# Four PSUM banks in one tile, one ScalarE copy for each unit, and eight absolute values moved from VectorE to ScalarE

## The chip, the core and the metric

The kernel runs on one core of one Trainium2 chip. A core has five engines that run side by side, each through its own list of instructions in order: TensorE (PE in the profile; its weight loads are PEld), VectorE (DVE), ScalarE (ACT), GpSimd (POOL) and SyncE (SP). They wait for each other through semaphores. The metric is the device time of one execution in microseconds (us): the median of three runs before was 1696.31 us (1691.14 to 1697.28).

## What is computed

One block with two parts, on 2048 tokens of width 576: a state-space convolution (the kernel of it is made from 128 complex poles for each channel, and applied by FFT), and a gated MLP.

```python
P = jnp.exp(logdA[:, :, None] * l[None, None, :])
K = jnp.einsum("dn,dnl,dn->dl", Cc, P, dB).real
...
Yf = Uf * Kf[None, :, :, :]
y = irfft2(Yf, (1, L2))[:, :, 0, :L] + u * Dskip
...
x = x + ga * _A_ref(h, ...)      # h: layer norm of x, modulated
h = _layernorm(x) * (1 + cb) + sb
z = gelu(h @ w_in); g = w_sp @ layernorm(z2) + b_sp
x = x + gb * ((z1 * g) @ w_out)
```

## The kernel before, in words

The function `ssm` makes the first part (about the first 385 us), `Mlp.phase_a` and `Mlp.phase_b` the second, a long stretch of float16 matrix products. The change touches `ssm` alone.

`ssm` is cut into small units, each a Python generator: a call runs it to its next `yield`, which records a few instructions on one or two engines. The text `ORDER` lists the calls, and nothing else sets the order: `t5 e9 k4` means the next step of `t_unit(5)`, `e_unit(9)`, `kg_unit(4)`. All instructions go through `Pin`, which keeps every engine in that order. The units:

- `poles` (O, P), `mod_unit` (M), `ln_stats` (S), `ln_rows` (R): the poles and the modulation rows, and the layer norm of the input. They stand early.
- `ln_half` (A, 16 of them): the first FFT step of half the channels of two token blocks. It writes four PSUM banks (`pk`), then copies each bank into `st1o`, 128 x 288, by a ScalarE instruction of its own (lines 552 to 554), with a `yield` behind each.
- `e_unit`, `t_unit`, `p_unit`, `kg_unit`, `k1_unit` (e, t, p, k, 1; 36 each): amplitudes (Exp), phases (Sin), their products on VectorE, the sum over poles on TensorE, and its first FFT step. In `t_unit` TensorE leaves phases in `ps` (two banks). For 25 of the 36 (`ROUNDED`) the rounding is done on TensorE; then VectorE takes the absolute value from PSUM into `ct` (line 603), ScalarE takes Sin of `ps` into `f`, and Sin of `ct` with a bias of a quarter turn. `p_unit` multiplies both on VectorE with the amplitudes.
- `u_unit`, `z_unit`, `v_unit`, `y_unit` (u, z, v, y): FFT of the input, the product in the frequency domain (VectorE), the way back, and the residual. `k1_unit` and `v_unit` write two banks and copy each by a ScalarE instruction of 128 x 256; `mod_unit` does so with 128 x 288, twice.

PSUM has eight banks. `ps` takes four, as two tiles of two banks. The other four are `pk_a` to `pk_d`, one tile each; `ps1()` hands them out, and the digits of `PLAN["pk"]` say which one comes next. A matmul that writes a bank waits until the last reader of that bank is done.

Of the kernel before, what the change touches and what calls it, by code (L numbers as in the profile page):

```python
# [9 lines left out]
F32 = mybir.dt.float32  # L10
# [4 lines left out]
ALU = mybir.AluOpType  # L15
# [15 lines left out]
COPIED = set()  # L31
# [6 lines left out]
    "pk": "01230123230123012301230120123012301231023102310232102130213021302130213021302301230122301230123012312031203120"  # L38
        "31203120312031203103201320323012302310231023103210321031203120132012031231201230123012032012031203120321021021"
        "30230123013021032103210321321031021032130130213021320123120312012301230123023102310231032103210123012301230213"  # L40
        "021320312031230123012310312031203120312031320120312031203123013021300101010101010101010101010101010101010101",
# [9 lines left out]
ON_ACT = set()  # L51
# [3 lines left out]
B0 O0 O0 O0 O0 B2 O0 O0 O0 O0 B7 O0 B1 O0 O0 O0 B6 O0 O0 O0 O0 O0 O0 x0 O0 O0 O0 O0 P0 S0 O0 S0 B3 O0 O0 i2 O0 O0 O0 P0 M2 O0 O0 S0 S0 B4 P0 S0 O0 Q0 P0 e1 S0 M2 e1 i1 e0  # L55
P0 P0 g0 e1 e0 P0 e0 e1 P0 t1 t2 i0 g1 O0 M2 e0 P0 M1 t1 t2 t1 P0 P0 t0 w3 P0 M1 t0 M2 t1 t0 t2 M1 M0 M1 M0 t0 e2 j1 R1 P0 p1 M3 t2 M0 p1 M3 R0 e2 R3 e6 p1 M0 B5 e2 M0 e6
M3 w4 k1 e4 e2 P0 M3 k1 O0 P0 e3 11 p0 e4 11 e6 M4 M0 e5 p0 P0 p0 e6 S1 S1 p2 M4 k0 M4 p2 11 R2 p2 e5 k0 e5 S1 M0 M3 M0 P0 k2 M4 e5 M0 P0 t5 k2 A0 e3 A0 S1 A0 A0 A0 w5 t5
S1 e3 P0 e3 A0 t3 S1 A1 t5 A1 A1 r2 A1 P0 t3 R4 A1 t7 A0 R5 A1 A2 A2 O0 P0 t3 t3 A2 A2 t4 P0 A1 A2 A2 A3 p3 A2 A3 t5 P0 r3 A3 A3 t4 t4 j2 M4 10 10 e4 A3 A3 A3 e4 12 p3 12
e7 p3 e7 P0 e7 R7 t7 10 R6 P0 p5 S2 12 k3 e8 e7 O0 k3 e8 A4 S2 A4 S2 A4 e8 S2 A4 A4 A4 e8 p5 P0 A5 t4 A5 A5 P0 A5 p5 A5 p4 A5 t7 a4 A4 A5 t6 A6 A6 A6 p4 A6 t6 A6 p4 A6 t8
A7 A7 P0 t7 A7 A7 O0 k4 A6 P0 S2 A7 13 t6 p7 A7 k4 t8 p7 R9 14 13 O0 k5 P0 P0 a5 t6 14 14 t8 p7 Q1 13 t8 M5 x3 k7 P0 e11 R8 A7 k5 M5 S3 k7 S3 A8 A8 e11 R11 e9 A8 e10 e11  # L60
P0 e9 e11 P0 p6 S3 S3 A8 P0 A8 R10 t10 A8 e10 A9 t10 A9 A9 A9 p8 p8 r6 e10 A9 A9 t9 e10 t10 A10 A8 P0 A10 A10 A10 A9 t11 p6 A10 A10 17 P0 t10 M5 p6 17 k6 M5 p8 t11 t9 17
k6 A11 A11 r7 S3 t11 t11 e12 A11 A11 Q2 15 R13 A11 A11 A10 p11 k8 t9 15 15 R12 A11 k8 A12 p11 A12 e12 A12 p11 A12 e14 A12 t14 A12 A13 e14 p10 A13 t14 A13 R15 e9 p10 A13
p10 A13 R14 A13 e9 t14 A12 e12 t12 e12 A14 A14 t9 A14 t15 A14 A14 t12 A13 t14 A14 t12 A15 A15 t14 O0 O0 A15 e16 k10 P0 A15 P0 A15 16 A15 P0 O0 p9 t12 k11 16 M5 p9 A14 A15
p9 C0 16 t14 18 c1 k10 f0 18 110 k11 18 110 e14 U2 110 U1 U0 t15 p12 111 t15 111 z2 111 t15 u2 t16 p12 u2 U5 p12 u0 e14 k9 c0 z2 z2 u0 k9 t16 k12 U4 p14 u1 19 U14 t16 U7
e16 k12 e15 19 t16 19 U23 e13 e15 e15 e16 u1 e15 c3 u7 e16 e13 p14 u4 u7 e13 u4 p14 c2 p15 z1 z1 e13 t13 U29 v2 u14 U6 t16 v2 p15 z4 U10 u14 t13 u6 t13 p15 t18 k15 z4 u6
u5 t16 k15 z1 p16 t18 p16 u29 e18 u5 U15 v1 z0 t13 u29 t18 e17 X1 t18 v1 U3 e18 115 115 u10 v1 v2 z0 u10 z0 X3 p16 e17 115 k14 k14 u3 b1 e17 e22 u3 p13 U12 e22 t17 e17
# [12 lines left out]
v29 k34 v18 p33 t32 v29 z27 134 X5 p33 W8 134 z28 t35 134 u34 u35 u34 z28 v27 u35 p35 v28 v27 p35 k33 z24 W11 v29 p35 v28 z31 p32 z24 z31 k33 133 133 k35 k35 y8 p32 v31
y8 133 p32 v27 z26 k32 z24 v31 135 k32 z26 132 z26 135 135 132 v24 v28 132 v31 W5 z34 v24 v26 D0 z35 L2 v26 v24 z34 L4 y5 v34 z35 L9 v34 y5 y8 L3 z25 z30 y5 L7 v35 z25  # L80
z25 u32 v35 u32 v25 z30 v25 L10 X19 L13 X11 v30 v26 L0 X17 X12 v25 z32 v30 L11 L20 v30 z33 z32 v32 X9 z33 v32 v33 v33 v34 W9 L12 L6 L1 v32 L14 v33 X13 y11 X10 X16 W13 y11
v35 y9 y13 W12 W10 W14 y12 L15 W16 y10 y13 L8 W17 L18 y12 y11 X14 W15 X15 W18 y9 y9 W19 y10 L19 y16 y16 y17 L22 y14 X18 y17 y15 y19 y18 y14 y12 y10 y15 y19 L16 y15 L17
y18 y16 y13 y17 y19 y14 y18
# [112 lines left out]
class Rings:  # L196
# [7 lines left out]
    def __call__(self, pool, shape, dt, name, bufs):  # L204
        if name not in self.plan:
            return pool.tile(shape, dt, name=name, bufs=bufs)
        if name not in self.tiles:
            self.tiles[name] = [pool.tile(shape, dt, name=f"{name}_{chr(97 + i)}", bufs=1) for i in range(bufs)]
        i = self.at[name]
        self.at[name] = i + 1  # L210
        return self.tiles[name][self.plan[name][i]]


class Pin:
# [5 lines left out]
    def __getattr__(self, name):  # L220
        f = getattr(self.engine, name)

        def call(*a, **k):
            return self.tc.keep_in_program_order(f(*a, **k))  # L224

        return call

# [9 lines left out]
def ssm(tc, I, x1_d, consts_s, dram, mod_d, mlp):  # L237
# [6 lines left out]
    with ExitStack() as ctx:  # L244
# [12 lines left out]

        def ps1():
            return ring(psp, [128, 512], F32, "pk", 4)
# [178 lines left out]
        def mod_unit(k):  # L438
            wm = wmt.pop(k)
            pm = [ps1(), ps1()]  # L440
            for hh in range(2):
                for kt in range(6):
                    j = (kt + 2 * hh) % 4
                    T.matmul(pm[hh][32 * j:32 * j + 32, :HC], ec[:, kt:kt + 1].to_broadcast([96, 32]),
                             wm[hh][:, kt], start=kt < 4, stop=kt >= 2, skip_group_check=True)
            yield
            mpart = ep.tile([128, D], F32, name="mpart", bufs=1)
            for hh in range(2):
                A.activation(v3(mpart)[:, hh], pm[hh][:, :HC], AF.Copy)
            yield  # L450
            pm = [ps1(), ps1()]
            for hh in range(2):
                T.matmul(pm[hh][:, :HC], ones, mpart[:, HC * hh:HC * hh + HC], start=True, stop=True)
            yield
            src = [t[:, :HC] for t in pm]
            if k == 2:
                for hh in range(2):
                    A.activation(v3(gar)[:, hh], src[hh], AF.Copy)
            elif k == 1:
                for hh in range(2):  # L460
                    V.scalar_tensor_tensor(v3(cga)[:, hh], src[hh], 1.0, v3(gar)[:, hh], op0=ALU.add, op1=ALU.mult)
# [2006 lines left out]
```

## Time and profile before

The execution that was profiled took 1691.0 us, of which its span (first to last instruction) is 1688.9 us.

| | PE | PEld | DVE | ACT | POOL |
|---|---|---|---|---|---|
| busy us of the span | 1615.6 | 1235.7 | 1298.4 | 873.8 | 209.7 |
| share | 96% | 73% | 77% | 52% | 12% |

The shares are means over very unlike stretches. The page cuts the span into 40 slices of 42 us and gives the busy share of each in tenths:

```profile
PE   3778999989999999999999999999999999999999
DVE  7898999867989877988997776894443487787555
ACT  6889999675776664555444433342321133353221
PEclk9978999999999999999999999999999999999999
```

The first eight or nine digits are `ssm`: VectorE and ScalarE stand at 8 or 9 in most of them. Behind it TensorE is at 9 to the end, and ScalarE falls to 1 to 5.

### The profile page before, as it was taken

How to read it: one execution, taken by the hardware profiler on the slowest of the kernel's cores; microseconds unless marked ns; L12 is line 12 of the kernel's file. 1: busy time of each engine (PE TensorE's matmuls, PEld its weight loads, DVE VectorE, ACT ScalarE, POOL GpSimd, SP SyncE). 2: the span in 40 equal slices, each digit the busy share in tenths (PEclk: the TensorE clock that was granted, in tenths of full speed). 3: DMA queues.
4: the chain of work that ended last, by engine and by line, in shares of the span. 5: the costliest groups of instructions: out<-in, count | busy, mean ns of one | idle time of the engine just before them, and what ended most of it. 6: DMA issues, size and time to landing. Idle time of an engine off the chain costs nothing.

```text
span 1688.9 us, 39922 instructions
## 1 busy us (share of the span) xinstructions
PE 1615.6 (96%) x16868; PEld 1235.7 (73%) x16868; DVE 1298.4 (77%) x2241; ACT 873.8 (52%) x1307; POOL 209.7 (12%) x340
## 2 busy tenths in 40 slices
PE   3778999989999999999999999999999999999999
PEld 1344677755555557778878888888888888888887
DVE  7898999867989877988997776894443487787555
ACT  6889999675776664555444433342321133353221
POOL 3251111112222110000000000000111100111100
PEclk9978999999999999999999999999999999999999
DMA  9667645596888898776738887664667573777560
GB/s 231 170 215 229 203 140 176 171 317 208 280 287 243 251 261 297 242 270 234 249 118 302 282 292 257 219 218 166 232 213 243 189 221 121 275 281 252 189 241 29
DMA packets 186402, 380.61 MB, mean 225 GB/s; under 512 B 38464, under 2 KB 105792, under 8 KB 185456
## 3 DMA queue, kind: packets, MB, share of 16 engines
q1 hardware_dynamic: 145216, 182.10, 35.2%
q0 software_dynamic: 34528, 169.11, 30.1%
q10 hardware_dynamic: 6480, 26.86, 3.9%
q8 instruction: 132, 2.16, 0.5%
q14 instruction: 46, 0.38, 0.1%
HBM read 272.73 MB, written 105.29 MB: 224 GB/s over the span
## 4 chain that ended last, share of the span: by engine, by line
PE 77%; DVE 7%; DMA 3%; issue 2%; ACT 2%; SPq 0%; POOL 0%; ACTq 0%; DVEq 0%; POOLq 0%
PE ps L224 58%; PE pz L224 10%; PE pk_b L224 2%; PE pk_a L224 2%; DMA zset<-set_d 2%; PE pk_c L224 2%; PE pk_d L224 1%; DVE zset L224 1%; DVE gt L224 1%; DVE bsz L224 1%; PE ps_a L224 0%; PE ps_b L224 0%; DMA v_d<-v_a 0%; PE pt L224 0%; DMA uu_a<-in_x 0%
## 5 line engine op out<-in xcount | busy, mean ns | idle before, releaser
L224 PEld LDWEIGHTS <-zset 128*128 128x128 f16 x7182 | 702.2, 98 | 86.5 <-DMA zset<-set_d 2.0
L224 PE MATMUL ps<-wsp,zset 128*128 128x256 f16 x6048 | 666.8, 273 | 2.2 <-DMA zset<-set_d 1.1
L224 PE MATMUL pz<-wz,nt 128*128 128x512 f16 (+1 forms) x1120 | 220.8, 358 | 1.5 <-ACT nt L224 1.0
L224 ACT ACTIVATE z<-gt 128x1024 f16<-128x1024 f32 x56 | 59.0, 1054 | 250.4 <-DVE gt L224 250.4
L224 PEld LDWEIGHTS <-nt 128*128 128x128 f16 x1120 | 109.4, 98 | 107.1 <-ACT nt L224 1.5
L2164 POOL DMA_DIRECT2D zset<-set_d x96 | 50.8, 529 | 862.5 <-PE ps L224 619.7
L224 PE MATMUL ps<-wout,z 128*128 128x288 f16 x1092 | 138.4, 286 | 0.0
L224 DVE SCALAR_TENSOR_TENSOR gt<-ps,sc,bsp 128x512 f32<-128x512 f32 x36 | 27.0, 749 | 143.0 <-PE ps L224 141.3
L224 PEld LDWEIGHTS <-z 128*128 128x128 f16 x1176 | 115.1, 98 | 28.9
L224 DVE TENSOR_TENSOR raw<-raw 128x256 f32<-128x256 f32 (+3 forms) x238 | 126.8, 539 | 7.7 <-DMA raw<-z_d 3.5
L224 PE MATMUL ps<-n2o,zset 128*128 128x256 f16 x1134 | 128.2, 273 | 0.0
L224 DVE SCALAR_TENSOR_TENSOR gt<-ps,sc,gt 128x512 f32<-128x512 f32 (+1 forms) x180 | 122.2, 696 | 7.6
L224 ACT ACTIVATE zset<-raw 128x1792 f16<-128x1792 f32 x48 | 81.1, 1691 | 59.3 <-PE ps L224 21.6
L224 DVE TENSOR_TENSOR zset<-raw,zset 128x1792 f16<-128x1792 f32 x48 | 96.9, 2020 | 15.7 <-ACT zset L224 15.7
L224 DVE TENSOR_TENSOR z<-ps,z 128x512 f32<-128x512 f32 (+1 forms) x126 | 72.0, 599 | 32.3 <-ACT z L224 25.9
L224 ACT ACTIVATE z<-pz,sc 128x512 f32<-128x512 f32 (+1 forms) x96 | 51.9, 574 | 39.9 <-PE pz L224 32.7
L224 ACT ACTIVATE wsp<-raw,sc 128x1792 f16<-128x1792 f32 x25 | 44.5, 1783 | 46.2 <-DVE raw L224 40.2
L224 ACT ACTIVATE z<-z,sc 128x1024 f32<-128x1024 f32 x21 | 24.1, 1148 | 76.0 <-DVE z L224 72.3
L224 ACT ACTIVATE z1b<-gt 128x512 f16<-128x512 f32 (+1 forms) x22 | 17.7, 821 | 84.0 <-DVE gt L224 84.0
L224 PE MATMUL ps<-n2q,wf 128*128 128x512 f16 x252 | 55.7, 379 | 0.0
L224 DVE BATCH_NORM_STATS2 bsz<-z 128x6 f32<-128x384 f32 x96 | 48.4, 548 | 5.0 <-ACT z L224 4.4
L224 DVE SCALAR_TENSOR_TENSOR wsp<-raw,sc,wsp 128x1792 f16<-128x1792 f32 x25 | 52.0, 2078 | 0.3 <-ACT wsp L224 0.3
(793 smaller groups left out, 2772.0 us busy)
## 6 DMA issues: line engine op xcount, KB each, us to landing
zset<-set_d POOLq DMA_DIRECT2D x96, 896.0 KB, 5.2
raw<-z_d SPq DMA_DIRECT2D x48, 512.0 KB, 5.6
set_d<-zset ACTq DMA_DIRECT2D x24, 896.0 KB, 6.4
z_d<-z POOLq DMA_DIRECT2D x32, 576.0 KB, 8.2
zset<-wa_d POOLq DMA_DIRECT2D x18, 896.0 KB, 4.9
raw<-in_w_spT SPq DMA_DIRECT2D x25, 512.0 KB, 4.4
set_d<-zset SPq DMA_DIRECT2D x12, 896.0 KB, 5.8
wst<-in_w_in SPq DMA_DIRECT2D x8, 1024.0 KB, 9.3
```

The costliest lines, as they stand in the source:

```text
L224: return self.tc.keep_in_program_order(f(*a, **k))
L2164: self.nc.gpsimd.dma_start(o, self.set_d[f, j - 1] if j else self.wa_d[f])
```

## The change

Three edits. `ORDER` has the same 1336 words.

1. The four tiles `pk_a` to `pk_d` become one tile, `banks`, of 128 x 4 x 512. `ps1()` returns one bank of it, and the new `psn(n)` returns n banks that lie side by side. Since a tile is now shared by work on different banks, `Pin.apart` tells the framework which pairs of a TensorE write and a read of another bank don't depend on each other. `PLAN["pk"]` has other digits, because the banks of a pair must be neighbours.
2. `ln_half`, `k1_unit`, `v_unit` and `mod_unit` copy all their banks by one ScalarE instruction, in the place of the first copy. The yields stay, so that the order of all else does. In `mod_unit` two VectorE pairs become one instruction each too.
3. `ON_ACT = {5, 7, 8, 10, 17, 21, 25, 29}`: in these eight `t_unit`s the absolute value of line 603 is taken by ScalarE (`AF.Abs`), in the same step.

```diff
-ON_ACT = set()
+ON_ACT = {5, 7, 8, 10, 17, 21, 25, 29}
...
+        banks = psp.tile([128, 4, 512], F32, name="banks", bufs=1)
+
         def ps1():
-            return ring(psp, [128, 512], F32, "pk", 4)
+            return banks[:, ring.take("pk")]
+
+        def psn(n):
+            i = min([ring.take("pk") for _ in range(n)])
+            return banks[:, i:i + n]
...
+    def apart(self, done, aps):
+
+        b = {x for ap in aps for x in banks_of(ap)}
+        if b:
+            names = {ap.tensor.name for ap in aps if hasattr(ap, "tensor")} - {ap.tensor.name for ap in aps if banks_of(ap)}
+            ins = getattr(done, "ins", done)
+            mine, others = (WRITES, READS) if self.engine is self.tc.nc.tensor else (READS, WRITES)
+            for c, i, n in others:
+                if not b & c and not names & n:
+                    self.tc.declare_no_dep(ins, i, reason="another bank")
+            mine.append((b, ins, names))
+        return done
...
-            pms = [ps1() for _ in range(4)]
+            pms = psn(4)
...
-            for g, pm in enumerate(pms):
-                A.activation(o[:, g], pm[:, :HC], AF.Copy)
+            A.activation(o, pms[:, :, :HC], AF.Copy)
+            for _ in range(4):
                 yield
...
-            for h in range(2):
-                pk = pm[h][:, :256].rearrange("p (c k) -> p k c", c=8)
-                if (g, h) in COPIED:
-                    V.tensor_copy(o[:, :, h], pk)
-                else:
-                    A.activation(o[:, :, h], pk, AF.Copy)
-                yield
+            A.activation(o, pm[:, :, :256].rearrange("p h (c k) -> p k h c", c=8), AF.Copy)
+            yield
+            yield
...
-            for q in range(2):
-                A.activation(v[:, 256 * q:256 * q + 256], pm[q][:, :256], AF.Copy)
+            A.activation(v.rearrange("p (q d) -> p q d", q=2), pm[:, :, :256], AF.Copy)
```

TensorE, GpSimd and SyncE have the same instructions in the same order. ScalarE has 1159 in place of 1281: 130 copies fewer (48 in `ln_half`, 36 in `k1_unit`, 36 in `v_unit`, 10 in `mod_unit`) and eight Abs more. VectorE has ten fewer. The table loads of ScalarE stay 30.

The first place is on ScalarE, in the middle of the `ln_half` units (about 107 to 112 us in the trace of before). `st1o_b` is the copy of an `ln_half`, `kab_a` and `k_a` are those of a `kg_unit` and a `k1_unit`, `ft_a` and `ft_b` the two phase tiles of `t_unit`s. Before, from the first copy on:

```order
L224 ACTIVATE st1o_b<-pk_a 128x288
L224 ACTIVATE st1o_b<-pk_c 128x288
L224 ACTIVATE st1o_b<-pk_b 128x288
L224 ACTIVATE ft_a<-ps_b 128x1024
L224 ACTIVATE st1o_b<-pk_d 128x288
L224 ACTIVATE kab_a<-pk_a 128x256
L224 ACTIVATE k_a<-pk_c 128x32x8
L224 DMA r1t<-in_c_r1t 128x128
L224 DMA cs<-in_c_cs 128x128
L224 ACTIVATE ft_a<-ft_a,consts_s 128x1024
L224 ACTIVATE k_a<-pk_d 128x32x8
L224 ACTIVATE k_a<-pk_a 128x32x8
```

And in the changed kernel:

```order
L227 ACTIVATE st1o_b<-banks 128x1152
L227 ACTIVATE ft_a<-ps_b 128x1024
L227 ACTIVATE kab_a<-banks 128x256
L227 ACTIVATE ft_b<-ps_a 128x1024
L227 ACTIVATE k_a<-banks 128x32x16
L227 DMA r1t<-in_c_r1t 128x128
L227 DMA cs<-in_c_cs 128x128
L227 ACTIVATE ft_a<-ft_a,consts_s 128x1024
L227 ACTIVATE k_a<-banks 128x32x16
L227 ACTIVATE ft_b<-ps_a 128x1024
```

The four copies of 288 columns are one of 1152, two of 256 are one of 512, and the first `ft_b<-ps_a` is the Abs of unit 8; the second is its Sin, which stood behind these rows before as well.

The second place is on VectorE, at about 231 us of the trace of before, where it goes from one product in the frequency domain (`zz`) to the next. Before:

```order
L224 TENSOR_TENSOR et_a<-ft_a,et_a 128x16x32
L224 TENSOR_SCALAR ft_b<-ps_a 128x1024
L224 TENSOR_SCALAR ft_c<-ft_c 128x1024
L224 TENSOR_TENSOR zz_a<-pk_c,uu_e 128x1024
L224 SCALAR_TENSOR_TENSOR ft_a<-ft_a,ps_b 128x1024
L224 TENSOR_TENSOR xb_a<-pk_a,xb_a 128x512
```

And now:

```order
L227 TENSOR_TENSOR et_a<-ft_a,et_a 128x16x32
L227 TENSOR_SCALAR ft_c<-ft_c 128x1024
L227 TENSOR_TENSOR zz_a<-banks,uu_e 128x1024
L227 SCALAR_TENSOR_TENSOR ft_a<-ft_a,ps_b 128x1024
L227 TENSOR_TENSOR xb_a<-banks,xb_a 128x512
```

One absolute value of 128 x 1024 is gone (that of unit 21), and all behind it moves up by one.

More of the change, by code (lines that the diff above doesn't have):

```diff
@@ L1 @@
 import math
+from collections import deque
 from contextlib import ExitStack
@@ L208, in __call__, with take @@
             self.tiles[name] = [pool.tile(shape, dt, name=f"{name}_{chr(97 + i)}", bufs=1) for i in range(bufs)]
+        return self.tiles[name][self.take(name)]
+    def take(self, name):
         i = self.at[name]
         self.at[name] = i + 1
[L211 removed]
+        return self.plan[name][i]
 class Pin:
@@ L223, in call, with banks_of @@
         def call(*a, **k):
-            return self.tc.keep_in_program_order(f(*a, **k))
+            return self.apart(self.tc.keep_in_program_order(f(*a, **k)), a + tuple(k.values()))
         return call
+    def apart(self, done, aps):
[9 more added lines that the diff above has]
+        return done
+READS, WRITES = deque(maxlen=48), deque(maxlen=320)
+def banks_of(ap):
+    t = getattr(ap, "tensor", None)
+    if t is None or not t.name.startswith("banks"):
+        return ()
+    at = {ap.offset % 2048}
+    for step, n in list(ap.ap)[1:]:
+        at = {o + step * j for o in at for j in (range(n) if step >= 512 else (0, n - 1))}
+    return {o // 512 for o in at}
 class Pinned:
@@ L447, in mod_unit @@
             mpart = ep.tile([128, D], F32, name="mpart", bufs=1)
+            A.activation(v3(mpart), pm[:, :, :HC], AF.Copy)
+            yield
+            pm = psn(2)
             for hh in range(2):
-                A.activation(v3(mpart)[:, hh], pm[hh][:, :HC], AF.Copy)
+                T.matmul(pm[:, hh, :HC], ones, mpart[:, HC * hh:HC * hh + HC], start=True, stop=True)
             yield
-            pm = [ps1(), ps1()]
-            for hh in range(2):
-                T.matmul(pm[hh][:, :HC], ones, mpart[:, HC * hh:HC * hh + HC], start=True, stop=True)
-            yield
-            src = [t[:, :HC] for t in pm]
+            src = pm[:, :, :HC]
             if k == 2:
-                for hh in range(2):
-                    A.activation(v3(gar)[:, hh], src[hh], AF.Copy)
+                A.activation(v3(gar), src, AF.Copy)
             elif k == 1:
-                for hh in range(2):
-                    V.scalar_tensor_tensor(v3(cga)[:, hh], src[hh], 1.0, v3(gar)[:, hh], op0=ALU.add, op1=ALU.mult)
+                V.scalar_tensor_tensor(v3(cga), src, 1.0, v3(gar), op0=ALU.add, op1=ALU.mult)
             elif k == 0:
-                for hh in range(2):
-                    V.tensor_tensor(v3(sga)[:, hh], src[hh], v3(gar)[:, hh], op=ALU.mult)
+                V.tensor_tensor(v3(sga), src, v3(gar), op=ALU.mult)
                 yield
@@ L473, in mod_unit @@
                 mrow = mpart if k == 4 else ep.tile([128, D], F32, name="gar", bufs=1)
-                for hh in range(2):
-                    if k == 4:
-                        A.activation(v3(mrow)[:, hh], src[hh], AF.Identity, bias=one)
-                    else:
-                        A.activation(v3(mrow)[:, hh], src[hh], AF.Copy)
+                if k == 4:
+                    A.activation(v3(mrow), src, AF.Identity, bias=one)
+                else:
+                    A.activation(v3(mrow), src, AF.Copy)
                 yield
@@ L548, in ln_half @@
                         rows = slice(32 * g, 32 * g + 32)
-                        T.matmul(pms[g][64 * t:64 * t + 64, :HC], x[rows], y[rows, c], start=st, stop=not st, skip_group_check=True)
+                        T.matmul(pms[64 * t:64 * t + 64, g, :HC], x[rows], y[rows, c], start=st, stop=not st, skip_group_check=True)
                 yield
             o = ring(ep, [128, 4, HC], F32, "st1o", 2)
-            for g, pm in enumerate(pms):
-                A.activation(o[:, g], pm[:, :HC], AF.Copy)
+            A.activation(o, pms[:, :, :HC], AF.Copy)
+            for _ in range(4):
                 yield
@@ L660, in k1_unit @@
                         s = slice(64 * h, 64 * h + 64)
-                        T.matmul(pm[h][64 * ri:64 * ri + 64, 64 * i:64 * i + 64], kk[s, i], r1[ri][s, s], start=True, stop=True,
+                        T.matmul(pm[64 * ri:64 * ri + 64, h, 64 * i:64 * i + 64], kk[s, i], r1[ri][s, s], start=True, stop=True,
                                  skip_group_check=True)
@@ L750, in v_unit @@
                     rows = slice(64 * q, 64 * q + 64)
-                    T.matmul(pm[q][:, :256], m[rows], zz[rows, k, 256 * r:256 * r + 256], start=not t, stop=t == len(terms) - 1,
+                    T.matmul(pm[:, q, :256], m[rows], zz[rows, k, 256 * r:256 * r + 256], start=not t, stop=t == len(terms) - 1,
                              skip_group_check=True)
```

78 lines of the change are left out of this document (38 added, 40 removed).

## The prediction

> **What bounds the kernel now.** The slices of the page say that the first 385 us are unlike the rest, so the first view to open is the one of busy time by stretch. I cut it where the engines' loads change.
>
> ```profile
> core 0: us, PE busy (x) PEld busy (x) DVE busy (x) ACT busy (x) POOL busy (x), PEclk, DMA share, GB/s
> 50.00:165.00 115.00, 90.71 (x2036) 49.63 (x2029) 105.81 (x189) 106.96 (x208) 41.20 (x64) 0.85 0.64 196
> 165.00:300.00 135.00, 130.59 (x2942) 94.33 (x2943) 131.73 (x170) 129.89 (x225) 20.32 (x35) 1.00 0.60 177
> 300.00:345.00 45.00, 44.78 (x966) 36.05 (x965) 37.23 (x53) 32.02 (x60) 8.78 (x13) 1.00 0.66 195
> 345.00:400.00 55.00, 46.08 (x416) 28.30 (x414) 34.60 (x78) 31.09 (x49) 12.55 (x19) 1.00 0.97 285
> 400.00:800.00 400.00, 399.70 (x2600) 255.01 (x2598) 347.27 (x741) 246.02 (x323) 49.84 (x64) 1.00 0.81 259
> ```
>
> In stage 1 (50 to 165 us) ScalarE is busy 106.96 of 115 us and VectorE 105.81: idle 8.04 and 9.19. In stage 2 (165 to 300) VectorE is idle 3.27 of 135, ScalarE 5.11, TensorE 4.41. So two engines are nearly full side by side, and neither is the bound alone. TensorE's 130.59 counts pipelined matmuls with modelled ends; its weight loads take 94.33 of 135, so I don't take it for full in stage 2. From 300 us on VectorE and ScalarE have room (7.77 and 12.98 of 45), and from 400 us on TensorE is busy 399.70 of 400.
>
> Next, how a gain in `ssm` reaches the end. The chain of work that ended last, between 340 and 390 us:
>
> ```profile
> 343.04 7.52 DMA v_d<-v_a
> ...
> 360.72 5.95 DMA v_d<-uu_d
> ...
> 372.21 6.88 DMA uu_a<-in_x
> ...
> 385.78 9.24 PE pz L224 x42
> ```
>
> It is a string of transfers and issues, which the change leaves alone, and then TensorE's matmuls of the second part, which follow each other to the end. It starts when `ssm`'s last units do: what stages 1 and 2 save, the whole execution saves, about one for one.
>
> **The change part by part.** First the copies. The busy times by which the page gives their cost overlap, so the price of one is the distance from its start to the next one's start, read where ScalarE doesn't wait. From ScalarE's timeline:
>
> ```profile
> 240.54 0.44 ACT L224 ACTIVATE k_a<-pk_b 128x256 f32<-128x256 f32 x1
> 240.81 0.45 ACT L224 ACTIVATE k_a<-pk_a 128x256 f32<-128x256 f32 x1
> 241.07 1.13 ACT L224 ACTIVATE ft_c<-ft_c 128x1024 f32<-128x1024 f32 x1
> 242.02 0.67 ACT L224 ACTIVATE uu_e<-pk_c 128x512 f32<-128x512 f32 x1
> 242.49 1.23 ACT L224 ACTIVATE ft_c<-ft_c,consts_s 128x1024 f32<-128x1024 f32 x1
> 243.53 0.68 ACT L224 ACTIVATE uu_c<-pk_b 128x512 f32<-128x512 f32 x1
> 244.01 1.11 ACT L224 ACTIVATE ft_b<-ps_a 128x1024 f32<-128x1024 f32 x1
> 244.91 0.48 ACT L224 ACTIVATE kab_b<-pk_d 128x256 f32<-128x256 f32 x1
> ```
>
> A copy of 256 columns takes 0.27 us (240.54 to 240.81), one of 512 takes 0.47, and an instruction of 1024 columns that reads the two banks of `ps` 0.90. Two of 256 cost 0.53 and one of 512 costs 0.47: a removed instruction is worth 0.06; from 512 to 1024 (0.47 twice against 0.90) it is 0.04. I take **0.05 us for each instruction that goes**. The durations beside the starts (0.44) tempt one to take 0.2. The four copies of an `ln_half`:
>
> ```profile
> 100.45 0.39 ACT L224 ACTIVATE st1o_b<-pk_a 128x288 f32<-128x288 f32 x1
> ...
> 101.32 0.42 ACT L224 ACTIVATE st1o_b<-pk_d 128x288 f32<-128x288 f32 x1
> 101.61 1.04 ACT L224 ACTIVATE ft_c<-ps_a 128x1024 f32<-128x1024 f32 x1
> ```
>
> They take 1.16 us (100.45 to 101.61); three instructions fewer leave 1.01 by an estimate from these rows. No row shows four banks read by one instruction: the ends are 1.16 (nothing saved) and 0.90 x 1152 / 1024 = 1.01 (slope alone, so the same as my value). That the merged copy of `k1_unit` reads with three steps costs nothing extra, as its parts, which read with two, take no more than others of their size.
>
> 130 copies go: 130 x 0.05 = 6.5 us of ScalarE's time over all of `ssm`, between 0 and 7.8 (at 0.06).
>
> The Trainium skill, page "ScalarE: Activation LUTs", section "What ACT_TABLE_LOAD costs", states 186 ns + 0.833 ns per column for an ACTIVATE with immediate scale and bias, and that back-to-back ones overlap by about 93 ns. So it would make a removed copy worth 93 ns, 12.1 us in all, and ScalarE's load would fall by some 5 us. The rows above contradict that: the second copy of 256 starts 0.27 us after the first, not 0.31.
>
> Second, the absolute values. VectorE's timeline has the first and the last of the eight:
>
> ```profile
> 73.15 1.22 DVE L224 TENSOR_SCALAR ft_a<-ps_a 128x1024 int32<-128x1024 int32 x1
> 74.28 0.60 DVE L224 SCALAR_TENSOR_TENSOR t_ph<-t_n_A_im,t_ph 128x432 f32<-128x432 f32 x1
> ...
> 284.20 1.21 DVE L224 TENSOR_SCALAR ft_b<-ps_a 128x1024 int32<-128x1024 int32 x1
> 285.33 1.21 DVE L224 TENSOR_TENSOR pg_a<-et_c,ft_c 128x1024 f32<-128x1024 f32 x1
> ```
>
> Each takes 1.13 us of VectorE, start to start: 8 x 1.13 = 9.0 us go from it, four in each stage (units 5, 7, 8, 10 before 165 us; 17, 21, 25, 29 behind it), 4.5 us each. ScalarE takes them over. Its Abs isn't in this trace; the nearest row is the Sin of the same tile from the same banks at 244.01, 0.90 us, and that value I take. The bounds: 0.90 below, since an instruction of that size is nowhere shorter, and 1.04 above (the Sin with a bias operand, 242.49 to 243.53). 8 x 0.90 = 7.2 us come to ScalarE, 3.6 in each stage. The number of table loads stays.
>
> Where the copies stand, counted by tile and stretch (ScalarE's instructions on `k_a`, `k_b`, `v_a`, `v_b` in stage 2, in this order):
>
> ```profile
> 165.00:300.00 135.00, 5.77 (x16) 1.00 0.60 177
> 165.00:300.00 135.00, 8.09 (x23) 1.00 0.60 177
> 165.00:300.00 135.00, 8.20 (x24) 1.00 0.60 177
> 165.00:300.00 135.00, 6.75 (x20) 1.00 0.60 177
> ```
>
> These are 83 copies of which half go: 41 x 0.05 = 2.1 us. With Abs, ScalarE's load in stage 2 rises by 3.6 - 2.1 = 1.5 us. In stage 1 stand all 16 `ln_half` (48 copies go) and, by the order, some 19 of the others that go (12 of `k1_unit`, 7 of `mod_unit`): 67 x 0.05 = 3.4, so its load there rises by 0.2 us. **ScalarE gains nothing from this change; VectorE loses 4.5 us in each stage.**
>
> Now the sum. In stage 2 ScalarE goes to 129.89 + 1.5 = 131.4 and VectorE to 131.73 - 4.5 = 127.2: ScalarE takes VectorE's place as the fullest, at almost the load that VectorE had. If it keeps the idle time that VectorE has now, 3.27, the stage takes 134.7 (gain 0.3); if it had no idle time at all, 131.4 (gain 3.6). Part of ScalarE's idle time is wait for TensorE, which waits for products of VectorE, so it shrinks as VectorE runs ahead; I take 1.5. In stage 1 ScalarE was the fullest already: 107.2 + 8.04 = 115.2 (loss 0.2) if its idle time stays, and 107.2 (gain 7.8) with none. Some of it stands outside VectorE's reach, as the waits in stage 1 show, ScalarE's first and then VectorE's longest:
>
> ```profile
> ACT kab_a L224 <- PE pk_b L224: 1.0, 1, 1.0
> ACT st1o_b L224 <- DMA u_d<-st1o_b: 1.0, 1, 1.0
> ACT st1o_a L224 <- PE pk_d L224: 0.7, 1, 0.7
> DVE pg_b L224 <- PE pk_c L224: 4.5, 1, 4.5
> ```
>
> I take 1.5 here too. Behind 300 us ScalarE is not the bound, and its last copies save nothing. Together 3.0 us: the profiled execution of 1691.0 us would be 1688.0. The runs shown have a median of 1696.31, 5.3 above it, within their own spread; from the median the forecast is **1693.3 us**. A measurement of this kernel tells about 0.5% (8.5 us) from no change, so this is "the same".
>
> **The rivals.** *ScalarE's waits go too.* If VectorE was what held the other two up, both stages shrink until ScalarE has next to no idle time: gain 3.6 + 7.8 = 11.4 at the most, and with a sixth of that left 9.5: 1686.8 us. For it: VectorE's idle time in stage 2 is the smallest, 3.27. Against: ScalarE's 5.11 leave little more, and the waits above lie on DMA and TensorE.
>
> *Banks come free later.* This is the rival on the slow side. All banks of a unit are now held until its one copy ends. In an `ln_half` the first bank was free after 0.39 us and is now after about 1.1 (1.01 and the overlap, an estimate), some 0.7 later; of a pair, after 0.67 instead of 0.44, some 0.2 later (the last bank comes free a little earlier). TensorE stood behind these copies before already; its waits in stage 1, and two of its matmuls right behind copies:
>
> ```profile
> PE pk_a L224 <- ACT st1o_b L224: 2.4, 2, 1.8
> PE pk_c L224 <- ACT st1o_b L224: 2.2, 3, 1.3
> 100.89 0.39 PE L224 MATMUL pk_a<-gsp,cs 32*64 32x288 bf16 x1 [1.77 <-ACT st1o_b L224]
> 107.04 0.29 PE L224 MATMUL pk_a<-dsk,small 128*32 128x4 f32 x8 [0.60 <-ACT st1o_b L224]
> ```
>
> At 100.89 the next `ln_half` starts as its first bank comes free, but it ends with its last bank, so the merged copy doesn't delay it. At 107.04 a `kg_unit` needs one bank only: there the 0.7 counts. The price if every unit did: 16 x 0.7 + 72 x 0.2 = 25.6 us. It decides from the point at which TensorE has no room: stage 2's 4.41 us of idle time by busy time, much more by weight loads. If half of it is exposed and the 3.0 gained, the time is 1696.3 + 12.8 - 3.0 = 1706.1 us.
>
> The Trainium skill, page "Perfetto Trace Analysis", section "Optimizing Tensor Performance" (Matmuls), speaks against the change in this sense: independent matmul groups should rotate through different PSUM banks, so that the evacuation of one overlaps the matmuls of the next. A unit that fills all four banks and is copied out by one instruction leaves no bank for the next group. By that rule this rival would be the case; the trace agrees for the wait at 107.04 and doesn't at 100.89.
>
> *The copies don't get cheaper.* If an instruction over several banks takes as long as its parts (the bound of 1.16 for 1.01), ScalarE gains 7.2 us of work and loses none. Stage 1 then costs 106.96 + 3.6 + 8.04, 3.6 more than now, and stage 2 133.5 + 3.27, 1.8 more, less what VectorE gives back: near 1699 us, still within 0.5%.
>
> **How the numbers follow.** The forecast (a change of a few us either way) 0.58, the copies that don't get cheaper 0.10, ScalarE's waits gone 0.18, banks later 0.14. The last one reaches 8.5 us only with nearly half of its price exposed, so 0.12 of it counts as slower; the rest goes to the same. Of the third 0.16 lies beyond 8.5. So: faster 0.16, the same 0.72, slower 0.12. The range reaches from 1685.5 (most of the fast case) to 1702 (half of the slow one's way), and takes in the runs' own spread of 3 us on each side.
>
> **What the new profile would show.** Copies of 1152 columns starting about 1.01 us before the next instruction, of 512 about 0.47, Abs 0.90. Between the same units, VectorE's busy time 9 us lower, ScalarE's within 1.5 us of now, and ScalarE's idle time between them about 3 to 5 us less. The chain from the last `v_d` store to the first `pz` as long as now. The forecast is wrong if TensorE's waits on `st1o` and on `k`, `v` copies grow by several us, if VectorE's gaps open at the eight places, or if ScalarE's idle time falls to nearly none.

## The result and the profile after

The changed kernel takes **1739.33 us** (median of 4 runs, 1738.71 to 1743.34), the kernel before beside it 1696.8 (4 runs). The ratio is 1.0262, with a 95% interval of 1.0235 to 1.029: 43 us slower, where 1693.3 was forecast and 1702 was the upper end of the range. The profiled execution, from its page (times in us, instructions behind the x):

```profile
span 1736.9 us, 39686 instructions
## 1 busy us (share of the span) xinstructions
PE 1628.6 (94%) x16868; PEld 1239.4 (71%) x16868; DVE 1291.4 (74%) x2231; ACT 877.3 (51%) x1185; POOL 209.8 (12%) x340
```

By busy time nothing speaks of 48 us more span (1688.9 before): VectorE is 7.0 us less busy (1298.4 before) and ScalarE 3.5 us more (873.8), both in the direction forecast. So the time is in gaps. First, what the prediction priced. From ScalarE's timeline of the changed kernel (start, duration, instruction, and in brackets the idle time ahead of it and what ended it):

```profile
106.08 1.13 ACT L227 ACTIVATE st1o_b<-banks 128x1152 f32<-128x1152 f32 x1 [0.60 <-PE banks L227]
107.10 1.02 ACT L227 ACTIVATE ft_a<-ps_b 128x1024 f32<-128x1024 f32 x1
...
109.65 1.02 ACT L227 ACTIVATE ft_b<-ps_a 128x1024 f32<-128x1024 f32 x1
...
110.55 0.60 ACT L227 ACTIVATE k_a<-banks 128x512 f32<-128x512 f32 x1
...
113.97 0.58 ACT L227 ACTIVATE k_a<-banks 128x512 f32<-128x512 f32 x1
114.45 1.01 ACT L227 ACTIVATE ft_b<-ps_a 128x1024 f32<-128x1024 f32 x1
```

Start to start, the merged copy of 1152 columns takes 1.02 us (106.08 to 107.10), the Abs of unit 8 takes 0.90 (109.65 to 110.55) and a merged pair 0.48 (113.97 to 114.45). The three prices are those of the prediction (1.01, 0.90, 0.47).

Now the two stages. They end at the same instructions as in the table of the prediction (165, 300 us), which are reached at about 174 and 337 us here:

```profile
core 0: us, PE busy (x) PEld busy (x) DVE busy (x) ACT busy (x) POOL busy (x), PEclk, DMA share, GB/s
50.00:174.00 124.00, 93.07 (x2031) 51.92 (x2024) 101.55 (x183) 106.62 (x146) 41.25 (x64) 0.78 0.60 182
174.00:337.00 163.00, 135.83 (x2906) 94.03 (x2906) 130.03 (x167) 132.91 (x186) 19.95 (x34) 0.97 0.49 146
```

Stage 2 has grown from 135 us to 163. VectorE is idle for 33.0 us of it (3.27 before) and ScalarE for 30.1 (5.11 before): both engines that were full now have gaps at once. The waits of the two between 175 and 340 us, longest groups first (us in total, times, longest), VectorE's and then ScalarE's:

```profile
DVE zz_b L227 <- ACT k_b L227: 5.8, 2, 3.5
DVE zz_a L227 <- ACT v_a L227: 5.0, 2, 2.9
DVE zz_a L227 <- PE banks L227: 3.9, 3, 1.9
...
DVE xb_a L227 <- ACT kab_b L227: 3.2, 2, 2.2
DVE xb_a L227 <- ACT k_b L227: 2.3, 1, 2.3
```

```profile
ACT kab_a L227 <- PE banks L227: 3.7, 3, 2.0
ACT v_a L227 <- DVE zz_b L227: 3.2, 1, 3.2
ACT v_b L227 <- DVE zz_b L227: 2.7, 2, 2.5
ACT v_a L227 <- DVE zz_a L227: 2.4, 1, 2.4
ACT et_e L227 <- DVE zz_a L227: 2.3, 1, 2.3
```

In the kernel before, VectorE's waits in stage 2 (165 to 300 us) are these three and no others:

```profile
DVE zz_a L224 <- PE pk_d L224: 1.6, 1, 1.6
DVE zz_b L224 <- PE pk_c L224: 0.9, 1, 0.9
DVE ft_b L224 <- ACT ft_b L224: 0.4, 1, 0.4
```

The new pairs make no sense as a flow of data. A product of `z_unit` (`zz`) doesn't read `k_b` or `v_a`, nor does the copy of a `v_unit` read the `zz` that it waits for. What the two sides share is the tile they read: `banks`. One such place, VectorE's timeline before, then VectorE's and ScalarE's in the changed kernel:

```profile
190.36 1.22 DVE L224 TENSOR_TENSOR zz_b<-pk_b,uu_g 128x1024 f32<-128x1024 f32 x1
191.50 0.68 DVE L224 TENSOR_SCALAR ft_a<-ft_a 128x1024 int32<-128x1024 int32 x1
192.10 1.23 DVE L224 TENSOR_TENSOR zz_a<-pk_d,uu_h 128x1024 f32<-128x1024 f32 x1
```

```profile
202.66 1.22 DVE L227 TENSOR_TENSOR zz_b<-banks,uu_g 128x1024 f32<-128x1024 f32 x1
203.80 0.68 DVE L227 TENSOR_SCALAR ft_a<-ft_a 128x1024 int32<-128x1024 int32 x1
207.42 1.23 DVE L227 TENSOR_TENSOR zz_a<-banks,uu_h 128x1024 f32<-128x1024 f32 x1 [2.94 <-ACT v_a L227]
```

```profile
203.97 0.60 ACT L227 ACTIVATE v_b<-banks 128x512 f32<-128x512 f32 x1 [2.47 <-DVE zz_b L227]
204.58 1.28 ACT L227 ACT_TABLE_LOAD   x1
205.88 1.02 ACT L227 ACTIVATE ft_c<-ps_a 128x1024 f32<-128x1024 f32 x1
206.80 0.59 ACT L227 ACTIVATE v_a<-banks 128x512 f32<-128x512 f32 x1
207.28 1.15 ACT L227 ACTIVATE ft_c<-ft_c,consts_s 128x1024 f32<-128x1024 f32 x1
```

ScalarE stood idle 2.47 us ahead of the copy of `v_b`, until VectorE had read another bank for `zz_b`; then VectorE stood idle 2.94 us until ScalarE had come through a table load, a Sin and the copy of `v_a`. The engines meet at such reads, each in turn waiting for the other. The waits in the changed kernel's instruction streams confirm it: 34 ScalarE reads of `banks` wait for a VectorE read of other banks, and 35 VectorE reads (27 products, six adds of `y_unit`, one in `mod_unit`, one copy in the second part) for a ScalarE read of other banks. Before, with four tiles, there is no wait of a read for a read of another bank, except where the one needs what the other wrote. `Pin.apart` declares a TensorE write independent of a read of another bank; it doesn't compare a read with a read, and the framework orders readers of one tile on different engines as the program has them.

That gives the theory, **readers wait for each other**, against two rivals: **banks come free later** (from the prediction) and **the eight Abs load ScalarE**.

### The profile page after: what moved, and what is told of

Same layout as the page of the kernel before. It is cut to its first block, busy times and chain, and to the rows that moved or that the text cites. A ratio compares the mean times of both kernels' runs of the same rounds, so it can differ in the third digit from the quotient of the medians.

```text
span 1736.9 us, 39686 instructions
## 1 busy us (share of the span) xinstructions
PE 1628.6 (94%) x16868; PEld 1239.4 (71%) x16868; DVE 1291.4 (74%) x2231; ACT 877.3 (51%) x1185; POOL 209.8 (12%) x340
## 4 chain that ended last, share of the span: by engine, by line
PE 65%; DVE 6%; DMA 5%; issue 2%; ACT 1%; SPq 0%; ACTq 0%; POOL 0%; DVEq 0%; POOLq 0%
PE ps L227 51%; PE pz L227 12%; DMA zset<-set_d 3%; PE banks L227 2%; DVE zset L227 2%; DVE gt L227 1%; DVE raw L227 1%; DMA v_d<-v_a 1%; DVE wsp L227 1%; PE pt L227 1%; DVE ot L227 0%; DMA wa_d<-zset 0%; DMA uu_a<-in_x 0%; DMA zz_a<-v_d 0%; ACT zset L227 0%
## 5 line engine op out<-in xcount | busy, mean ns | idle before, releaser
L227 ACT ACTIVATE wsp<-raw,sc 128x1792 f16<-128x1792 f32 x25 | 44.5, 1784 | 46.2 <-DVE raw L227 40.2
```

Source lines behind the costliest of these rows:

```text
L227: return self.apart(self.tc.keep_in_program_order(f(*a, **k)), a + tuple(k.values()))
```

## The experiments

Ratios are to the kernel before on the same chip, with 95% intervals; they can differ from the quotient of two medians by about 0.1% (2 us). Experiments 1 to 4 ran on one chip, 5 to 8 on another, 9 to 11 on a third, 12 alone, 13 to 15 together and 16 alone: between these groups the ratios compare, the medians less well. "Readers independent" means the edit of the first experiment. Where the same instruction stands in the main runs' profiles, in us later than in the profile of before:

| start before | changed | tile alone | changed, readers independent | tile, readers independent |
|---|---|---|---|---|
| 113.9 | -0.7 | -0.7 | 2.3 | -0.9 |
| 164.9 | 8.7 | 3.2 | 12.2 | 3.2 |
| 202.9 | 15.3 | 10.6 | 13.5 | 5.7 |
| 252.6 | 25.5 | 20.6 | 20.1 | 6.3 |
| 303.7 | 37.6 | 35.3 | 21.8 | 7.9 |
| 353.5 | 46.2 | 44.1 | 25.4 | 8.5 |
| 403.1 | 46.9 | 46.0 | 25.3 | 7.1 |

The last column is the measure of the rest: that kernel has the median of the kernel before, but the one profile of before is an execution of 1691.0 us, at the fast end of its runs.

**1. The changed kernel, readers independent.**

```diff
-            mine, others = (WRITES, READS) if self.engine is self.tc.nc.tensor else (READS, WRITES)
-            for c, i, n in others:
+            te = self.engine is self.tc.nc.tensor
+            mine, others = (WRITES, READS) if te else (READS, WRITES)
+            for c, i, n, e in list(others) + [r for r in READS if not te and r[3] is not self.engine]:
                 if not b & c and not names & n:
                     self.tc.declare_no_dep(ins, i, reason="another bank")
-            mine.append((b, ins, names))
+            mine.append((b, ins, names, self.engine))
```

> The changed kernel, with one thing undone in its waits: a VectorE and a ScalarE instruction that read different banks of the tile `banks` are declared independent of each other. In the changed kernel 34 ScalarE reads wait for a VectorE read of other banks and 35 VectorE reads for a ScalarE read of other banks; here none does. Orders, merged copies, bank plan and the eight Abs stay. Theory 'readers wait for each other': these rendezvous cost the steady loss of 175 to 335 us (about 36 us), and only the loss of 125 to 165 us (about 9 us) is left, which the prediction's gain of 3 may reduce: 1695 to 1708 us, the gaps of VectorE behind ScalarE's copies at the z products are gone. Rival 'banks come free later' (one copy holds two or four banks until its end): TensorE's waits stay, 1733 to 1743 us. Rival 'the eight Abs load ScalarE': 1733 to 1743 us.

Measured: 1713.7 us, ratio 1.0123 (1.0103 to 1.0143). Of the 43 us some 25 are gone by this edit alone (25.6 by the medians, 24 by the ratios). The same product as above, in VectorE's timeline, and the two stages (columns as in the table of stages above):

```profile
205.10 0.69 DVE L227 TENSOR_SCALAR ft_a<-ft_a 128x1024 int32<-128x1024 int32 x1
205.70 1.22 DVE L227 TENSOR_TENSOR zz_a<-banks,uu_h 128x1024 f32<-128x1024 f32 x1
```

```profile
50.00:177.00 127.00, 96.92 (x2016) 54.18 (x2013) 97.91 (x178) 105.95 (x143) 41.26 (x64) 0.74 0.58 175
177.00:322.00 145.00, 133.12 (x2946) 93.42 (x2944) 129.54 (x168) 132.74 (x189) 20.48 (x35) 0.99 0.54 165
```

`zz_a` follows at once, and stage 2 takes 145 us in the place of 163. But the time is above the 1695 to 1708 expected: something else costs some 19 us.

**2. Only the Abs**, in the kernel before.

```diff
-ON_ACT = set()
+ON_ACT = {5, 7, 8, 10, 17, 21, 25, 29}
```

> The kernel before, with the eight absolute values of the rounded phases on ScalarE and nothing else changed (four tiles, copies apart). Theory 'readers wait for each other': no such wait is here, so 1690 to 1700 us. Rival 'the eight Abs load ScalarE' (8 x 0.90 = 7.2 us more on it, none taken off by merged copies): up to 7 us if ScalarE bounds both stages, 1700 to 1704 us; more than that, up to 1739 us, only if the Abs are the cause of the loss.

Measured: 1697.43 us, ratio 1.0018 (1.0003 to 1.0032): some 3 us slower, not the cause of 43. Stage 2 of this run (its boundaries stand at 169 and 311 us):

```profile
169.00:311.00 142.00, 133.47 (x2956) 96.19 (x2955) 128.66 (x167) 134.61 (x231) 20.50 (x35) 0.99 0.57 169
```

VectorE is idle for 13.3 us, ScalarE for 7.4. (The execution that was profiled is the slowest of this kernel's twelve, 1702.64 us.)

**3. Only the tile**: the kernel before with the one tile `banks` and the changed kernel's `Pin.apart`; copies apart, old plan, no Abs.

```diff
+        banks = psp.tile([128, 4, 512], F32, name="banks", bufs=1)
+
         def ps1():
-            return ring(psp, [128, 512], F32, "pk", 4)
+            return banks[:, ring.take("pk")]
...
```

> The kernel before, with its four bank tiles made one tile `banks`, and the changed kernel's declarations (a TensorE write and a read of another bank are independent); copies apart, the bank plan and the Abs as before. All engines have the orders of before, and TensorE's waits are those of before but for a handful. 35 ScalarE reads wait for a VectorE read of other banks, and 36 VectorE reads for a ScalarE read of other banks. Theory 'readers wait for each other': it alone has most of the loss, about 36 us of it from 175 to 335 us: 1725 to 1738 us. Rival 'banks come free later': no copy is merged and the plan is the old one, so 1693 to 1700 us. Rival 'the eight Abs': 1693 to 1700 us.

Measured: 1735.13 us, ratio 1.0237 (1.0207 to 1.0267). The tile by itself loses 40 us, with none of the merged copies.

**4. The tile, readers independent**: experiment 3 with the edit of experiment 1.

> The run before this one (one tile, copies apart, old plan, no Abs) with the readers of different banks declared independent too: in the built program ScalarE, VectorE and TensorE wait as in the kernel before but for eight places. Theory 'readers wait for each other': 1693 to 1700 us, and the difference to the run with the tile alone is the price of those waits. If something else about the single tile costs the time (its place in PSUM, say), it stays with the run before this one, 1725 to 1738 us. Rivals 'banks come free later' and 'the eight Abs': 1693 to 1700 us, like the run before.

Measured: 1694.59 us, ratio 0.9999 (0.9983 to 1.0015): the kernel before. Stage 2 of experiments 3 and 4:

```profile
168.00:335.00 167.00, 142.34 (x2942) 99.04 (x2941) 133.39 (x171) 132.13 (x224) 19.96 (x34) 0.95 0.48 143
```

```profile
168.00:308.00 140.00, 134.53 (x2954) 96.54 (x2953) 132.15 (x171) 131.45 (x228) 20.47 (x35) 0.98 0.57 171
```

The same instructions with the same busy times on VectorE and ScalarE (133.39 against 132.15, 132.13 against 131.45) take 167 us or 140. The two differ in the waits between readers and in nothing else, so these waits are the price: **40.5 us alone, and some 25 beside the rest of the change**, where part of their idle time would probably be there anyway (no run shows which part).

**5 to 8. What is left: Abs, merged copies, or the new plan.** All four start from experiment 1 (1713.7 us). Without the Abs (`ON_ACT = set()`):

> The changed kernel with its readers of different banks independent (the run of 1713.7 us), and the eight absolute values back on VectorE. What is left of the loss there is 19 us. Theory 'banks come free later' for what is left: the Abs have little part in it, 1709 to 1715 us (alone they cost 2.6 us). Rival 'the eight Abs' for what is left: 1695 to 1702 us.

With each bank copied by itself at its old step, in all units and then in `ln_half` alone (the edit in `ln_half`; the other units have the like):

```diff
-            A.activation(o, pms[:, :, :HC], AF.Copy)
-            for _ in range(4):
+            for g in range(4):
+                A.activation(o[:, g], pms[:, g, :HC], AF.Copy)
                 yield
```

> The same kernel (readers of different banks independent, Abs on ScalarE, the new bank plan with neighbour banks), but each bank copied out by an instruction of its own at its old step, in all four kinds of unit. Theory 'one copy holds all its banks until its end': the 19 us are gone, 1694 to 1702 us. Rival 'the new plan's choice of banks is the cause' (neighbours have to be free together, and other units get the bank that came free last): 1708 to 1717 us, as with merged copies. In between, both have a share.

> The same kernel with merged copies, except in ln_half, where four copies of 288 columns stand in the place of one of 1152, at their old steps. Theory 'one copy holds all its banks', with its price mostly at the four banks (a copy of 1.0 us, behind which the next unit's first matmul waits; TensorE's waits for these copies are the largest group there, 14.7 us): 1697 to 1705 us. Rival 'the plan', or 'the pairs': 1708 to 1716 us.

And in all but `ln_half`:

> The counterpart: one copy of 1152 columns in ln_half, while k1_unit, v_unit and mod_unit copy each bank by itself. Theory 'one copy holds all its banks', mostly at the four banks: 1706 to 1713 us. Rival 'the pairs hold the banks': 1696 to 1703 us. Rival 'the plan': 1708 to 1716 us.

Measured: without Abs 1711.74, ratio 1.0093 (1.0059 to 1.0127); all apart 1711.07, 1.0089 (1.0068 to 1.0109); `ln_half` apart 1711.14, 1.0083 (1.0051 to 1.0116); the others apart 1714.3, 1.0109 (1.0081 to 1.0137). None comes back to 1700, and the last three lie where the rival 'the plan' had them. The second and third compute other values, though: the new plan gives a bank to its next user from the merged copy's step on, so a copy of `ln_half` at a later step reads what that user wrote. They have other dependencies than a kernel that computes the right values, and their times are hints only. The fourth is sound: copying pairs apart doesn't bring back the 19 us.

**9. The old plan with merged copies.** `psn` takes the banks by the plan of before, one instruction where they are neighbours, else one for each, at one step. All of `ln_half`'s copies merge and 47 of the other 82 that the change takes away. Within a unit the banks are taken from the lowest up, which the plan of before doesn't do.

```diff
-            i = min([ring.take("pk") for _ in range(n)])
-            return banks[:, i:i + n]
+            i = sorted([ring.take("pk") for _ in range(n)])
...
+            cut = range(1) if i[-1] - i[0] == n - 1 else range(n)
+            return [(banks[:, i[k]:i[k] + n // len(cut)], slice(k, k + n // len(cut))) for k in cut]
```

> The changed kernel with its readers of different banks independent, Abs on ScalarE, and the bank plan of before in the place of the new one. Every ln_half has all four banks there and copies them by one instruction; a pair copies both banks by one instruction where the old plan gives neighbours, else by two, one right behind the other: 95 of the 130 copies go. Theory 'the new plan's choice of banks costs the 19 us that are left': 1690 to 1700 us. Rival 'a merged copy holds its banks until its end': 1706 to 1716 us, since all four-bank copies and most pairs are merged.

Measured: 1706.45 us, ratio 1.0075 (1.0055 to 1.0096): above what 'plan' gave, at the lower end of what its rival gave. It is 7 us below experiment 1 and 12 above experiment 4, so neither theory has the whole.

**10. The same without the Abs.**

> The run before this one with the eight absolute values back on VectorE: copies merged where the old plan lets them be, nothing else of the change. Theory 'plan': 1688 to 1698 us; the 95 copies that are gone, at 0.05 us each, are 4.8 us of ScalarE, of which the prediction's reasoning would let 1 to 4 us reach the end. Rival 'a merged copy holds its banks': 1706 to 1716 us.

Measured: 1700.87 us, ratio 1.0042 (1.0024 to 1.0061). This lies between the two theories' ranges. Against experiment 4, 95 copies fewer make the kernel slower, by 6 us (7 by the ratios).

**11. The new plan, copies apart at one step.** A unit's copies stand one behind the other in the place of the merged one.

> The new plan again (readers independent, Abs on ScalarE), with each bank copied by an instruction of its own, all copies of a unit at the step of the merged one, one right behind the other; so each bank's contents are safe, as they were not in the two runs where copies stood at their old, later steps under the new plan. Theory 'plan': 1708 to 1716 us, like merged copies. Rival 'a merged copy holds its banks until its end': the first banks of a unit come free earlier, 1696 to 1704 us.

Measured: 1711.08 us, ratio 1.0095 (1.007 to 1.012), in the range of 'plan'. Against experiment 1, banks that come free one by one bring 2.6 us by the medians and 5 by the ratios, whose intervals overlap. Most of the loss stays with the new plan.

**12 to 14. Four banks or pairs.** From experiment 4 (one tile, readers independent, old plan, no Abs): the pairs merged and `ln_half` as before. The first version takes `ln_half`'s banks in the order of their numbers instead of the plan's order, and so reads some after their next user's write; it computes other values, and its time is a hint only:

> One tile, readers of different banks independent, the bank plan of before, no Abs on ScalarE; in ln_half four copies of 288 columns at their old steps, as in the kernel before. Only the pairs of k1_unit, v_unit and mod_unit are copied by one instruction where the old plan gives neighbours (47 of their 82 copies that the change takes away go). Theory 'the four-bank copy holds its banks': with all merged it was 6 us over the run without any; that is the price of ln_half, and the pairs bring up to 47 x 0.05 = 2.4 us: 1691 to 1696 us. Rival 'the pairs cost the 6 us': 1699 to 1703 us.

Measured: 1698.37 us, ratio 1.0022 (1.0005 to 1.0039). Then with the plan's order:

```diff
-            (pms, _), = psn(4)
+            pms = [ps1() for _ in range(4)]
...
```

> As the run before (one tile, readers independent, old plan, no Abs, neighbour pairs merged, ln_half in four copies at its old steps), with the four copies in the order in which the old plan takes the banks, so that each bank is read before its next user writes it. Theory 'the four-bank copy holds its banks': the pairs bring up to 2.4 us against the run with nothing merged (1694.6), 1691 to 1696 us. Rival 'the pairs cost too': 1697 to 1702 us.

Measured: 1697.77 us, ratio 1.0019 (1.0005 to 1.0033). The counterpart, `ln_half` merged alone:

> The counterpart: one tile, readers independent, old plan, no Abs, every pair in two copies at its old steps, and only ln_half copied by one instruction of 1152 columns (48 copies fewer). Theory 'the four-bank copy holds its banks': 1698 to 1703 us, TensorE's waits for these copies near the 19.3 us that they have with the pairs merged too, against 8.9 us with nothing merged. Rival 'the pairs cost the 6 us': 1692 to 1696 us.

Measured: 1699.62 us, ratio 1.0027 (1.0013 to 1.0042). By the ratios both cost something, and neither gains: the pairs 3 us, where they were to bring 2.4, the four-bank copy 5. TensorE's waits for the four-bank copies are 14.2 us (rows below), not the 19.3 expected.

**15 and 16. Why the four-bank copy costs.** Experiment 14 with the one instruction cut into four at the same step, then the same with the banks in the plan's order:

```diff
-            A.activation(o, pms[:, :, :HC], AF.Copy)
+            for g in range(4):
+                A.activation(o[:, g], pms[:, g, :HC], AF.Copy)
             for _ in range(4):
                 yield
```

> The run before this one with ln_half's one instruction cut into four of 288 columns at the same step, one right behind the other (so ScalarE works at these copies as early as with one instruction, 0.15 us longer, but each bank is free when its own copy ends). If the price is that all four banks are held until one instruction ends: 1692 to 1697 us. If it is that the work of four steps stands in one step, ahead of what stood between: 1698 to 1703 us, like the one instruction.

> One tile, readers independent, old plan, no Abs, pairs apart at their old steps; ln_half's four copies of 288 columns all at the step of the first, in the order in which the old plan takes the banks. It differs from the run where the four copies stand at one step (1699.8 us) only in that the banks are not taken from the lowest up, as one instruction over four banks has to, and from the run with nothing merged (1694.6 us) only in the place of the copies on ScalarE. If the place costs the 5 us: 1698 to 1703 us. If the order of the banks within the unit costs them (the next unit's first bank is then not the one that came free first): 1692 to 1697 us.

Measured: 1699.81 us, ratio 1.0038 (1.0022 to 1.0053), and 1698.15 us, ratio 1.0013 (0.9998 to 1.0028). TensorE's waits for these copies, 50 to 180 us, with one instruction (experiment 14), with four at one step (15), and with these in the plan's order (16):

```profile
PE banks L228 <- ACT st1o_b L228: 10.1, 7, 1.8
PE banks L228 <- ACT st1o_a L228: 4.1, 5, 1.4
```

```profile
PE banks L228 <- ACT st1o_b L228: 8.2, 6, 1.9
PE banks L228 <- ACT st1o_a L228: 2.2, 3, 1.5
```

```profile
PE banks L228 <- ACT st1o_b L228: 8.7, 7, 2.9
PE banks L228 <- ACT st1o_a L228: 1.3, 2, 0.7
```

Four instructions shorten these waits by 3.8 us (14.2 to 10.4) and the kernel isn't faster. So holding four banks until one instruction ends is not what costs the 5 us. Two causes are left: the place (the work of four steps stands in one) and the order (one instruction over neighbours needs the banks from the lowest up). The times don't divide the 5 us between them: by the ratios the order costs 4 us and the place 2, with intervals that overlap a little (1.0022 to 1.0028), while the median of experiment 16, 1698.15, lies at the lower end of what 'the place' gave.

The profiles speak for the order, and say where: the instruction that ended stage 1 at 164.9 us before starts at 173.2 us in experiment 15 and 172.6 in 14, but at 167.7 in 16 and 168.1 in experiment 4. Experiment 16 then gives 4 of these 5.5 us back further on (one profile of each). TensorE's waits for the copies are as long in 16 as in 15 (10.0 and 10.4 us), so what the order costs isn't in them; in which wait it is stays open.

## Why the prediction was wrong

**What bounds the kernel** held: two engines nearly full side by side, neither the bound alone. So a wait of one for the other finds little idle time to hide in. What `ssm` loses the end loses, one for one: 46.2 us at the instruction that stood at 353.5 us, 46.9 at 403.1, and 48.0 over the span.

**The prices** held: 1.02 for 1.01, 0.48 for 0.47, 0.90 for 0.90 us. So the rival "the copies don't get cheaper" falls. By the figures of the Trainium skill's page "ScalarE: Activation LUTs" ("What ACT_TABLE_LOAD costs"), 186 ns for each ACTIVATE beside its columns and 93 ns of overlap in a row, a removed copy is worth 93 ns by estimate, nearly twice the 0.04 to 0.06 us that the rows show.

**The step that failed** is the list of parts itself. The prediction priced the copies and the Abs, and the tile `banks`, the first of the three edits, had no price. It looked for new waits among TensorE's alone (its slow rival is "Banks come free later"); `Pin.apart` too speaks of TensorE's writes alone. The runs show in its place: making four tiles one orders VectorE's and ScalarE's reads, 69 waits of the kind that `Pin.apart` doesn't lift, 40.5 us alone and some 25 of the 43 here (experiments 1, 3 and 4). The built program has them to be read before the run: the waits of each engine for each other engine, not TensorE's alone.

**The sum of the stages**, gain 3.0, had the wrong sign for a second reason, since without the readers' waits the kernel is still 19 us slower (experiment 1). The sum took 1.5 us of gain in each stage, though ScalarE's load rises: its idle time had to shrink, by 3.0 us in stage 2 and 1.7 in stage 1, as VectorE runs ahead. With the whole change and readers independent (experiment 1) ScalarE is idle for 12.3 us of stage 2 and 21.1 of stage 1; with the tile alone (experiment 4) for 8.6 and 11.2. The term "it shrinks as VectorE runs ahead" has the wrong sign there. With the Abs alone (experiment 2) its idle time in stage 2 does shrink, to 7.4 us, but by less than the 3.2 us that its work grows (134.61 against 131.45), and VectorE's relief becomes VectorE's idle time (13.3 against 7.9). The merged copies that were to pay for the Abs don't pay: with the readers' waits, the Abs and the new plan taken away, the kernels with fewer copies are 3 to 6 us slower (experiments 10, 13 and 14).

**The rival "Banks come free later"** named a real loss with a wrong mechanism. Its sign did show: TensorE's waits for the copies of `ln_half` (50 to 180 us) are 15.2 us in the changed kernel and 8.5 before. Its 1706.1 us is also near what the merged copies, the Abs and the plan cost without the readers' waits, 1706 to 1714 (experiments 9 and 1), but that is luck: freeing the banks one by one brings nothing that can be told from the spread (experiments 11 and 15), so by these runs the holding isn't the greater part. The rule of the Trainium skill's page "Perfetto Trace Analysis" ("Optimizing Tensor Performance"), to rotate independent matmul groups through different banks, gives no price, and these two experiments show none that is clear of the spread.

What the 19 us are made of, by medians and then by ratios: merged copies on the old plan 6 or 7 (experiment 10 against 4), the Abs 6 there (9 against 10), and 7 or 8 for the new plan with the other 35 copies merged (1 against 9). This holds along one path only: the Abs cost 3 by themselves (experiment 2) and 2 or 5 under the new plan (1 against 5). Why the new plan's choice of banks costs what it does stays open, and for the pairs too only their price is known.

**"ScalarE's waits go too"** fell: ScalarE's gaps grew (30.1 us of stage 2 against 5.11).

No version here beats the kernel before. The best is that kernel on one tile with readers independent, which takes the same time (ratio 0.9999).

## What to carry to other kernels

When buffers are made one, ask for each pair of engines, readers against readers too, which order the framework now imposes, and count the waits in the instruction streams before pricing anything else. Here two engines that were both nearly full turned the false waits into idle time on both sides, in turn. A copy that is cheaper by itself need not be cheaper in place: a merged one does the work of several steps in one and needs its banks side by side and in order, which cost more here than the 0.05 us that each removed copy saves.

## What was unexpected

Two engines can lose 40 us by waits for each other over which no byte passes: 27 of it lie in a stage in which VectorE's and ScalarE's busy times are the same within 1.3 us (167 against 140 us). And the clock that TensorE is granted in the first 170 us differs between kernels with nearly the same work there: 0.85 in the profile of before (50 to 165 us) and 0.79 in that of experiment 4 (50 to 168):

```profile
50.00:168.00 118.00, 96.19 (x2036) 51.94 (x2029) 105.98 (x188) 106.81 (x207) 41.21 (x64) 0.79 0.63 192
```

The second reaches the end of stage 1 3.2 us later, though the medians of the two kernels agree. So a loss of a few us in that stretch, read from one profile of each, isn't yet an effect of a change; the 8.7 us at 164.9 us in the changed kernel may hold some of this. The clock alone doesn't set the time of the stretch, though: in experiment 10 it is 0.85 as well, and the end of stage 1 comes 9.3 us later than before.
